# Reordering the prologue of a fused attention and feed-forward kernel: load queues, weights, cluster chain in halves, spread squares, and the place of a normalisation

## The chip, the cores and the metric

The kernel runs on one core of one Trainium2 chip. The metric is the device time of one execution in microseconds (us). A run's "span" comes from its profile and is some 2 us shorter than its time. The profile also gives the mean clock that TensorE was granted, as a share of full speed. Engines in the profile: PE is TensorE (PEld its weight loads), DVE is VectorE, ACT is ScalarE, POOL is GpSimd, SPq is the issuing queue of SyncE, ACTq that of ScalarE.

## The reference, cut to what matters

```python
# q, k, v: 4 batches x 8 heads x 768 positions x 64; 16 centroids per head
q_assign = argmax(q_n @ c_n, clusters);  k_assign = argmax(k_n @ c_n, clusters)
scores   = where(q_assign == k_assign, q @ k.T / 8, -1e9)
x        = softmax(scores) @ v                      # -> 3072 rows of 512
xn       = x / sqrt(mean(x * x) + 1e-6) * rms_g
out      = (silu(xn @ w_gate) * (xn @ w_val)) @ w_out   # 512 -> 1536 -> 512
```

## The kernel before

The kernel keeps q and k transposed, with extra rows below the 64 of the head: 16 rows that mark the position's cluster (one-hot), and one constant row. One product then gives score plus mask. `trans` transposes on TensorE, copies on ScalarE and casts on VectorE and GpSimd. `scores_c` finds the cluster of every position on VectorE and sends the one-hot rows into place by eight small DMAs for a group of four heads.

```python
def load(n):                       # all from SyncE: q, k, v of one head
    ...
    nc.sync.dma_start(out=qk[:, :, 0], in_=src(q))
    nc.sync.dma_start(out=qk[:, :, 1], in_=src(k))
    nc.sync.dma_start(out=vs, in_=src(v))

def trans(g, h, part):
    ...                            # 3 transposes, copy to qkT (one buffer)
    if part:
        nc.gpsimd.tensor_copy(qext[g % 4][:D, h], qkT[g][:D, h])
        nc.vector.tensor_scalar_mul(kext[g % 4][:D, h], qkT[g][D:, h], 1.0 / ZS)
        nc.gpsimd.tensor_copy(vbf[g % 4][:, h, :, :D], vs)
        load(g * HG + h + NSTG)    # the next load, before the rows of oh below

def scores_c(g, m):
    ...                            # 4 products, transpose, max, is_equal, transpose -> oh
        for h in range(HG):
            nc.sync.dma_start(out=qext[g % 4][D:D + NC, h], in_=oh[32 * h:32 * h + NC])
            nc.sync.dma_start(out=kext[g % 4][D:D + NC, h], in_=oh[32 * h + NC:32 * h + 2 * NC])

def rms(u):                        # normalisation of a unit
    for t in range(HT):            # 3 squares with a sum, 512 columns, on ScalarE
        nc.scalar.activation(junk, x[:, t], ACT.Square, accum_out=ss[:, t:t + 1])
    ...                            # 12 tiny VectorE operations: 1/sqrt by Newton
    for t in range(HT):
        nc.vector.tensor_scalar_mul(xn[u][:, t], x[:, t], y[:, t:t + 1])
```

The body is a loop over eight units of half a batch. Between the 24 score steps of unit u it works off a list: the output product of unit u-2, then the feed-forward part of u-1, with the transposes of a later group mixed in.

```python
def ffn_work(u):
    w = [(0.18, lambda c=c: xtrans(u, c)) for c in range(CC)]   # transposes of xn
    ...                                                         # gate and value products
...
for u in range(NU):
    ...
    for h in range(H):
        for i in range(3):
            scores(u, h, i)                                     # 2 products, one exp
            if i == 0 and (u, h) != (0, 0):
                pv(u, h - 1) if h else pv(u - 1, H - 1)
                if h == 0:
                    rms(u - 1)                                  # at the unit's start
            ...                                                 # take from the list
```

The softmax here doesn't subtract the row's maximum and nothing guards it: scores larger than these inputs give would overflow.

## Time and profile before

| | before |
|---|---|
| time, median of 3 runs before the change was measured | 423.85 us (419.03 to 425.24) |
| span of the profiled run, granted clock | 422.2 us, 0.931 |
| first score product | 53.18 us |
| last product of unit 0 with v | 81.2 us |
| first gate product | 90.45 us |
| end of the last unit's products with v (start of the next product) | 381.74 us |

The four instants cut the span into five parts: a prologue to the first scores, unit 0, the wait for the first normalised rows, a body of 291.3 us (90.45 to 381.74) and a tail of 40.5 us. The body holds units 1 to 7. The profile's own lines are in the prediction.

### The profile page before, as it was taken

How to read it: one execution, taken by the hardware profiler on the slowest of the kernel's cores; microseconds unless marked ns; L12 is line 12 of the kernel's file. 1: busy time of each engine (PE TensorE's matmuls, PEld its weight loads, DVE VectorE, ACT ScalarE, POOL GpSimd, SP SyncE). 2: the span in 40 equal slices, each digit the busy share in tenths (PEclk: the TensorE clock that was granted, in tenths of full speed). 3: DMA queues.
4: the chain of work that ended last, by engine and by line, in shares of the span. 5: the costliest groups of instructions: out<-in, count | busy, mean ns of one | idle time of the engine just before them, and what ended most of it. 6: DMA issues, size and time to landing. Idle time of an engine off the chain costs nothing.

```text
span 422.2 us, 7646 instructions
## 1 busy us (share of the span) xinstructions
PE 354.2 (84%) x2995; PEld 213.8 (51%) x3009; DVE 232.4 (55%) x509; ACT 237.7 (56%) x404; POOL 59.6 (14%) x85
## 2 busy tenths in 40 slices
PE   3701188579997999799988999799979999999896
PEld 2301136346754665456635665466546665664452
DVE  4500133555674666756766668567765656666341
ACT  3300259838855676557745774677656675674230
POOL 3840305102110121002300211013100000000000
PEclk9965559869998999999999999999999999999899
DMA  7999985604222233014312220200011001000101
GB/s 188 202 207 207 221 186 144 158 12 98 71 57 70 81 94 79 19 76 110 84 40 89 63 51 2 70 25 2 2 44 50 2 2 75 2 2 13 63 0 75
DMA packets 63795, 32.03 MB, mean 76 GB/s; under 512 B 52976, under 2 KB 59664, under 8 KB 63760
## 3 DMA queue, kind: packets, MB, share of 16 engines
q1 hardware_dynamic: 61024, 26.83, 25.0%
q0 software_dynamic: 2736, 4.72, 6.1%
q8 instruction: 23, 0.38, 0.4%
q14 instruction: 12, 0.10, 0.1%
HBM read 28.35 MB, written 6.29 MB: 82 GB/s over the span
## 4 chain that ended last, share of the span: by engine, by line
PE 69%; DMA 9%; DVE 7%; ACT 6%; SPq 4%; issue 3%; POOL 0%; DVEq 0%; ACTq 0%
PE gate L275 15%; PE val L275 14%; PE s L205 13%; PE o L299 11%; PE acc L221 8%; DMA qk<-in_k_dram 6%; PE tq L160 4%; ACT pT L207 3%; ACT junk L237 2%; PE sc L177 2%; SPq L80 1%; PE tx L264 1%; DVE o_sb L302 1%; DMA vs<-in_v_dram 1%; SPq L81 1%
## 5 line engine op out<-in xcount | busy, mean ns | idle before, releaser
L207 ACT ACTIVATE pT<-s 128x768 bf16<-128x768 f32 x192 | 153.7, 811 | 63.0 <-PE s L205 61.8
L205 PE MATMUL s<-qext,kext 81*128 81x384 bf16 x384 | 96.1, 334 | 17.0 <-issue 7.5
L275 PE MATMUL gate<-xnT,wg 128*128 128x384 bf16 x384 | 80.4, 330 | 0.0
L275 PE MATMUL val<-xnT,wv 128*128 128x384 bf16 x384 | 79.1, 328 | 0.0
L285 DVE SCALAR_TENSOR_TENSOR gu<-th,gate 128x384 f32<-128x384 f32 x84 | 46.5, 553 | 54.0 <-ACT th L283 53.5
L299 PE MATMUL o<-wo,gvT 128*128 128x512 bf16 x274 | 70.5, 388 | 0.8
L163 POOL CAST qext<-qkT 64x768 bf16<-64x768 f32 x32 | 33.9, 1061 | 236.4 <-ACT qkT L161 236.4
L205 PEld LDWEIGHTS <-kext 81*128 81x128 bf16 x384 | 35.9, 99 | 54.5 <-issue 28.3
L160 PE MATMUL tq<-ident_f,qk 128*128 128x128 f32 x192 | 35.5, 308 | 31.2 <-DMA qk<-in_k_dram 30.8
L161 ACT COPY qkT<-tq 128x384 f32<-128x384 f32 x64 | 30.5, 481 | 50.7 <-PE tq L160 49.7
L221 PEld LDWEIGHTS <-pT 128*128 128x128 bf16 x1152 | 46.9, 99 | 12.6 <-ACT pT L207 3.5
L221 PE MATMUL acc<-vbf,pT 128*128 128x65 bf16 x1152 | 50.6, 195 | 2.0 <-ACT pT L207 1.5
L283 ACT ACTIVATE th<-gate 128x384 f32<-128x384 f32 x84 | 41.1, 489 | 19.9 <-PE gate L275 19.9
L290 DVE SCALAR_TENSOR_TENSOR gvT<-gu,val 128x384 bf16<-128x384 f32 x84 | 46.5, 554 | 9.5 <-PE val L275 3.1
L275 PEld LDWEIGHTS <-wv 128*128 128x128 bf16 x384 | 36.7, 98 | 23.1 <-issue 1.4
L275 PEld LDWEIGHTS <-wg 128*128 128x128 bf16 x384 | 36.5, 98 | 22.7 <-issue 1.9
L164 DVE TENSOR_SCALAR kext<-qkT 64x768 bf16<-64x768 f32 x32 | 23.2, 729 | 43.3 <-ACT qkT L161 42.2
L160 PEld LDWEIGHTS tq<-ident_f,qk 128*128 128x128 f32 x192 | 25.9, 157 | 39.8 <-issue 30.1
L299 PEld LDWEIGHTS <-gvT 128*128 128x128 bf16 x288 | 27.3, 99 | 28.5 <-issue 2.6
L237 ACT ACTIVATE junk<-x 128x512 bf16<-128x512 f32 x24 | 15.1, 629 | 18.7 <-DVE x L227 18.2
L302 DVE COPY o_sb<-o 128x512 f32<-128x512 f32 x24 | 16.1, 687 | 11.4 <-PE o L299 9.5
L165 POOL CAST vbf<-vs 128x384 bf16<-128x384 f32 x32 | 18.7, 584 | 0.0
(53 smaller groups left out, 165.0 us busy)
## 6 DMA issues: line engine op xcount, KB each, us to landing
qk<-in_q_dram SPq DMA_DIRECT2D x32, 192.0 KB
qk<-in_k_dram SPq DMA_DIRECT2D x32, 192.0 KB
vs<-in_v_dram SPq DMA_DIRECT2D x32, 192.0 KB
out_dram<-o_sb SPq DMA_DIRECT2D x24, 256.0 KB
wg<-in_moe_w_gate_dram POOLq DMA_DIRECT2D x4, 384.0 KB, 9.0
wv<-in_moe_w_val_dram POOLq DMA_DIRECT2D x4, 384.0 KB, 10.5
wo<-in_moe_w_out_dram POOLq DMA_DIRECT2D x3, 512.0 KB, 19.1
qext<-oh SPq DMA_DIRECT2D x32, 24.0 KB
```

The lines of the kernel that those rows point to most:

```text
L160: nc.tensor.transpose(ps[:, i * P:(i + 1) * P], qk[:, t].rearrange("p a d -> p (a d)"), ident_f)
L161: nc.scalar.copy(qkT[g][:, h, part * UQ:(part + 1) * UQ], ps)
L163: nc.gpsimd.tensor_copy(qext[g % 4][:D, h], qkT[g][:D, h])
L205: nc.tensor.matmul(ps[:, j, :UQ], lhsT=kext[g % 4][:KR, hh, kc * P:(kc + 1) * P], rhs=qext[g % 4][:KR, hh, hf * UQ:(hf + 1) * UQ], start=T ...
L207: nc.scalar.activation(pT[u, h][:, 2 * i:2 * i + 2], ps[:, :, :UQ], ACT.Exp, scale=scale * ZS)
L221: nc.tensor.matmul(acc[:, h % 2, t], lhsT=pT[u, h][:, kc, t * P:(t + 1) * P], rhs=vbf[g % 4][:, hh, kc], start=kc == 0, stop=kc == ST - 1)
L237: nc.scalar.activation(junk, x[:, t], ACT.Square, accum_out=ss[:, t:t + 1])
L275: nc.tensor.matmul(ps, lhsT=w[:, c, f * P:(f + 1) * P], rhs=xnT[u][:, c], start=c == 0, stop=c == CC - 1)
L283: nc.scalar.activation(th, ps, ACT.Tanh, scale=0.5)
L285: nc.vector.scalar_tensor_tensor(gu, th, 1.0, ps, op0=ALU.add, op1=ALU.mult)
L290: nc.vector.scalar_tensor_tensor(gvT[u][:, f], gates[u], 0.5, ps, op0=ALU.mult, op1=ALU.mult)
L299: nc.tensor.matmul(outs[u], lhsT=gvT[u][:, f, t * P:(t + 1) * P], rhs=wo[:, f], start=f == 0, stop=f == FC - 1)
```

## The change

It means to end the 30 us in which TensorE waits for loads, and to take the squares out of the exps' way. Its parts:

1. q and k of the first heads first, k and the first v from ScalarE's queue; later loads after the cluster rows; weights in pieces.
2. The first group's cluster chain in two halves of two heads.
3. The constant row becomes exp's bias: 80 rows, eight small DMAs less.
4. The squares' first 384 columns move between the last head's exps. The rest, and the whole normalisation, move from the unit's start to the list, just ahead of the transposes of xn.
5. Eight dummy products at the very start.

```diff
-        nc.sync.dma_start(out=qk[:, :, 0], in_=src(q))
-        nc.sync.dma_start(out=qk[:, :, 1], in_=src(k))
-        nc.sync.dma_start(out=vs, in_=src(v))
+    nc.sync.dma_start(out=staged[n][:, :, 0], in_=src(q, n))
+    (kq or nc.sync).dma_start(out=staged[n][:, :, 1], in_=src(k, n))
 ...
+    for n in range(HG):
+        load_qk(n, nc.scalar)
+    for n in range(HG, NQ):
+        load_qk(n)
+    for n in range(HG):
+        load_v(n, nc.scalar)
 ...
+    for i in range(WARM):
+        nc.tensor.matmul(warm_ps[:, i % 2], lhsT=warm[:, :P], rhs=warm, start=True, stop=True)
 ...
-    nc.scalar.activation(pT[u, h][...], ps[:, :, :UQ], ACT.Exp, scale=scale * ZS)
+    nc.scalar.activation(pT[u, h][...], ps[:, :, :UQ], ACT.Exp, bias=off, scale=scale * ZS)
 ... (squares(u, t, last): 384 columns early, 128 in rms)
-        w = [(0.18, lambda c=c: xtrans(u, c)) for c in range(CC)]
+        w = [(0.0, lambda: rms(u))] + [(0.18, lambda c=c: xtrans(u, c)) for c in range(CC)]
 ...
+        if h % 2:
+            for m in range(2):
+                scores_c(0, m, h - 1, h + 1)
 ...
+    load_gv(1)
+    load_gv(3)
     for u in range(NU):
 ...
+            def more():
+                for c in range(0, FC, 4):
+                    load_o(c)
+                for n in range(H, H + NV):
+                    if n < H + NQ:
+                        load_qk(n)
+                    load_v(n)
+            fill = first[4:] + [(0.0, more)] + prep
+        elif u == 1:
+            fill = prep[:4] + spread(ffn_work(0), prep[4:])
 ...
-                    if h == 0:
-                        rms(u - 1)
+                if h == H - 1:
+                    squares(u, i, False)
```

More of the change, by code (lines that the diff above doesn't have):

```diff
@@ L50 @@
     scale = 1.0 / (D ** 0.5)
-    KR = D + NC + 1
-    NSTG = 6
+    KR = D + NC
+    WARM = 8
+    NQ, NV = 6, 8
     ctx.enter_context(tc.manual_schedule())
@@ L56 @@
     const = pool("const", 1)
-    stage = pool("stage", NSTG)
+    stage = pool("stage", NQ)
     qk32 = pool("qk32", 1)
@@ L67, with src, load_qk, load_v @@
     ps_g = pool("ps_g", 3, space=PSUM)
-    staged = {}
-    def load(n):
+    staged, stagedv = {}, {}
+    def src(a, n):
+        b, h = divmod(n, H)
+        return a[b, h].rearrange("(p t) d -> p t d", t=ST)
+    def load_qk(n, kq=None):
         if n >= B * H:
             return
-        b, h = divmod(n, H)
-        qk = stage.tile([P, ST, 2, D], F32, tag="qk", name="qk")
-        vs = stage.tile([P, ST, D], F32, tag="vs", name="vs")
-        src = lambda a: a[b, h].rearrange("(p t) d -> p t d", t=ST)
-        nc.sync.dma_start(out=qk[:, :, 0], in_=src(q))
-        nc.sync.dma_start(out=qk[:, :, 1], in_=src(k))
-        nc.sync.dma_start(out=vs, in_=src(v))
-        staged[n] = (qk, vs)
+        staged[n] = stage.tile([P, ST, 2, D], F32, tag="qk", name="qk")
+        nc.sync.dma_start(out=staged[n][:, :, 0], in_=src(q, n))
+        (kq or nc.sync).dma_start(out=staged[n][:, :, 1], in_=src(k, n))
+    def load_v(n, vq=None):
+        if n >= B * H:
+            return
+        stagedv[n] = stage.tile([P, ST, D], F32, tag="vs", name="vs", bufs=NV)
+        (vq or nc.sync).dma_start(out=stagedv[n], in_=src(v, n))
     c_in = const.tile([P, D], F32)
     nc.sync.dma_start(out=c_in, in_=centroids.rearrange("h c d -> (h c) d"))
-    for n in range(NSTG):
-        load(n)
-    gcol = const.tile([P, CC], F32)
-    nc.sync.dma_start(out=gcol, in_=moe_rms_g.rearrange("(c p) -> p c", p=P), allow_slow_non_contiguous=True)
+    for n in range(HG):
[4 more added lines that the diff above has]
+        load_v(n, nc.scalar)
+    gcol = const.tile([P, CC], F32)
+    warm = const.tile([P, 512], BF16)
+    nc.vector.memset(warm, 1.0)
+    warm_ps = ps_s.tile([P, 2, 512], F32, tag="s", name="warm")
+    for i in range(WARM):
+        nc.tensor.matmul(warm_ps[:, i % 2], lhsT=warm[:, :P], rhs=warm, start=True, stop=True)
     ones = const.tile([P, P], F32)
@@ L108 @@
     kext = [const.tile([P, HG, S], BF16, name=f"kext{i}") for i in range(4)]
-    cq = const.tile([1, S], BF16)
-    ck = const.tile([1, S], BF16)
-    nc.gpsimd.memset(cq, -1.0)
-    nc.gpsimd.memset(ck, 1.0)
-    for i in range(4):
-        nc.sync.dma_start(out=qext[i][KR - 1:KR], in_=cq.unsqueeze(1).broadcast_to([1, HG, S]))
-        nc.sync.dma_start(out=kext[i][KR - 1:KR], in_=ck.unsqueeze(1).broadcast_to([1, HG, S]))
     vbf = [const.tile([P, HG, ST, D + 1], BF16, name=f"vbf{i}") for i in range(4)]
@@ L118 @@
         nc.gpsimd.memset(vbf[i][:, :, :, D:D + 1], 1.0)
+    off = const.tile([P, 1], F32)
+    nc.gpsimd.memset(off, -scale * ZS)
     c_sq = const.tile([P, D], F32)
@@ L141, with load_gv, load_o @@
     wo = const.tile([P, FC, DM], BF16)
-    def load_weights():
-        for c in range(CC):
-            nc.gpsimd.dma_start(out=wg[:, c], in_=moe_w_gate[c * P:(c + 1) * P])
-            nc.gpsimd.dma_start(out=wv[:, c], in_=moe_w_val[c * P:(c + 1) * P])
-        for c in range(0, FC, 4):
-            nc.gpsimd.dma_start(out=wo[:, c:c + 4], in_=moe_w_out[c * P:(c + 4) * P].rearrange("(c p) f -> p c f", p=P))
+    def load_gv(c):
+        nc.gpsimd.dma_start(out=wg[:, c], in_=moe_w_gate[c * P:(c + 1) * P])
+        nc.gpsimd.dma_start(out=wv[:, c], in_=moe_w_val[c * P:(c + 1) * P])
+    def load_o(c):
+        nc.gpsimd.dma_start(out=wo[:, c:c + 4], in_=moe_w_out[c * P:(c + 4) * P].rearrange("(c p) f -> p c f", p=P))
     qkT = {}
@@ L155, in trans @@
             qkT[g] = qk32.tile([P, HG, S], F32, tag="qkT", name="qkT")
-        qk, vs = staged[g * HG + h]
+        qk = staged[g * HG + h]
         ps = ps_g.tile([P, UQ], F32, tag="gen", name="tq")
@@ L164, in trans, with vcast @@
             nc.vector.tensor_scalar_mul(kext[g % 4][:D, h], qkT[g][D:, h], 1.0 / ZS)
-            nc.gpsimd.tensor_copy(vbf[g % 4][:, h, :, :D], vs)
-            load(g * HG + h + NSTG)
+    def vcast(n):
+        nc.gpsimd.tensor_copy(vbf[n // HG % 4][:, n % HG, :, :D], stagedv[n])
     scT = {}
-    def scores_c(g, m):
-        if m == 0:
-            scT[g] = asg.tile([P, S], F32, tag="scT", name="scT")
-        ps = ps_g.tile([P, UQ], F32, tag="gen", name="sc")
-        h0 = g * HG % H
-        for h in range(HG):
-            nc.tensor.matmul(ps[32 * h:32 * h + 32], lhsT=cblk[:, h0 + h], rhs=qkT[g][:, h, m * UQ:(m + 1) * UQ],
-                             start=True, stop=True)
-        nc.vector.transpose(scT[g][:, m * UQ:(m + 1) * UQ], ps)
-        if m:
-            n = 2 * S // 32
-            cl = scT[g].rearrange("p (n c) -> p n c", c=NC)
-            mx = small.tile([P, n], F32, tag="mx", name="mx")
-            nc.vector.tensor_reduce(mx, cl, axis=AX, op=ALU.max)
-            ohT = asg.tile([P, S], BF16, tag="ohT", name="ohT")
-            nc.vector.tensor_tensor(ohT.rearrange("p (n c) -> p n c", c=NC), cl,
-                                    mx.unsqueeze(2).broadcast_to([P, n, NC]), op=ALU.is_equal)
-            oh = asg.tile([P, S], BF16, tag="oh", name="oh")
-            nc.vector.transpose(oh, ohT)
-            for h in range(HG):
@@ new lines, with scores_c @@
+    ohs = {}
+    def scores_c(g, m, h0=0, h1=HG):
+        ps = ps_g.tile([P, UQ], F32, tag="gen", name="sc")
+        r = slice(32 * h0, 32 * h1)
+        for h in range(h0, h1):
+            nc.tensor.matmul(ps[32 * h:32 * h + 32], lhsT=cblk[:, g * HG % H + h],
+                             rhs=qkT[g][:, h, m * UQ:(m + 1) * UQ], start=True, stop=True)
+        sct = asg.tile([P, UQ], F32, tag="scT", name="scT", bufs=2)
+        nc.vector.transpose(sct[r], ps[r])
+        n = UQ // NC
+        cl = sct[r].rearrange("p (n c) -> p n c", c=NC)
+        mx = small.tile([P, n], F32, tag="mx", name="mx")
+        nc.vector.tensor_reduce(mx[r], cl, axis=AX, op=ALU.max)
+        ohT = asg.tile([P, UQ], BF16, tag="ohT", name="ohT", bufs=2)
+        nc.vector.tensor_tensor(ohT[r].rearrange("p (n c) -> p n c", c=NC), cl,
+                                mx[r].unsqueeze(2).broadcast_to([32 * (h1 - h0), n, NC]), op=ALU.is_equal)
+        if m == 0:
+            ohs[g, h0] = asg.tile([P, S], BF16, tag="oh", name="oh", bufs=2)
+        oh = ohs[g, h0]
+        nc.vector.transpose(oh[r, m * UQ:(m + 1) * UQ], ohT[r])
+        if m:
+            for h in range(h0, h1):
@@ L206, in scores @@
                              rhs=qext[g % 4][:KR, hh, hf * UQ:(hf + 1) * UQ], start=True, stop=True)
-        nc.scalar.activation(pT[u, h][:, 2 * i:2 * i + 2], ps[:, :, :UQ], ACT.Exp, scale=scale * ZS)
+        nc.scalar.activation(pT[u, h][:, 2 * i:2 * i + 2], ps[:, :, :UQ], ACT.Exp, bias=off, scale=scale * ZS)
     xs, accs = {}, {}
@@ L230, with squares @@
     xn = {}
+    sq = {}
+    def squares(u, t, last):
+        if (t, last) == (0, False):
+            sq[u] = small.tile([P, 2, HT], F32, tag="ss", name="ss")
+        c = slice(DM - 2 * D, DM) if last else slice(0, DM - 2 * D)
+        junk = ffn.tile([P, DM], BF16, tag="junk", name="junk", bufs=1)
+        nc.scalar.activation(junk[:, c], xs[u][:, t, c], ACT.Square, accum_out=sq[u][:, int(last), t:t + 1])
     def rms(u):
         x = xs[u]
-        ss = small.tile([P, HT], F32, tag="ss", name="ss")
         for t in range(HT):
-            junk = ffn.tile([P, DM], BF16, tag="junk", name="junk", bufs=1)
-            nc.scalar.activation(junk, x[:, t], ACT.Square, accum_out=ss[:, t:t + 1])
+            squares(u, t, True)
+        ss = small.tile([P, HT], F32, tag="sm", name="sm")
+        nc.vector.tensor_add(ss, sq[u][:, 0], sq[u][:, 1])
         ms = small.tile([P, HT], F32, tag="ms", name="ms")
@@ L304, in out_mm, with group_work, second @@
             nc.sync.dma_start(out=rows[:, hf * HT + t], in_=o)
-    def group_work(g):
+    def group_work(g, loads=True):
         w = []
         for h in range(HG):
-            for part in range(2):
-                w.append((0.25, lambda h=h, part=part: trans(g, h, part)))
+            n = g * HG + h
+            w.append((0.25, lambda h=h: trans(g, h, 0)))
+            def second(h=h, n=n):
+                trans(g, h, 1)
+                vcast(n)
+                if loads:
+                    load_qk(n + NQ)
+                    load_v(n + NV)
+            w.append((0.25, second))
         for m in range(2):
@@ L336, in out_work @@
         return [(0.86, lambda t=t, p=p: out_mm(u, t, p)) for t in range(HT) for p in range(3)]
-    for _, f in group_work(0):
-        f()
-    load_weights()
-    for _, f in group_work(1)[:2 * HG]:
-        f()
+    for h in range(HG):
+        for part in range(2):
+            trans(0, h, part)
+        if NQ + h < H:
+            load_qk(NQ + h)
+        if h % 2:
+            for m in range(2):
+                scores_c(0, m, h - 1, h + 1)
+    for n in range(HG, H):
+        load_v(n)
+    for h in range(HG):
+        vcast(h)
+        if h % 2:
+            load_gv(h - 1)
+    nc.sync.dma_start(out=gcol, in_=moe_rms_g.rearrange("(c p) -> p c", p=P), allow_slow_non_contiguous=True)
+    first = group_work(1, False)
+    for _, f in first[:4]:
+        f()
+    load_gv(1)
+    load_gv(3)
     for u in range(NU):
@@ L347 @@
             fill += out_work(u - 2)
-        prep = []
+        prep = group_work(u + 2) if u + 2 < NG else []
         if u == 0:
-            fill = group_work(1)[2 * HG:]
-            prep = group_work(2)
-        elif u + 2 < NG:
-            prep = group_work(u + 2)
-        fill += spread(ffn_work(u - 1), prep) if u >= 1 else prep
+            def more():
[4 more added lines that the diff above has]
+                        load_qk(n)
+                    load_v(n)
+            fill = first[4:] + [(0.0, more)] + prep
+        elif u == 1:
+            fill = prep[:4] + spread(ffn_work(0), prep[4:])
+        else:
+            fill += spread(ffn_work(u - 1), prep)
         total = sum(c for c, _ in fill)
@@ L370 @@
     pv(NU - 1, H - 1)
-    rms(NU - 1)
     for _, f in out_work(NU - 2) + ffn_work(NU - 1) + out_work(NU - 1):
```

## The prediction

> **What bounds the kernel now.** I read the page first (busy shares, slices, chain), then the work of the engines in chosen stretches, then the timeline of three places where TensorE stands still.
>
> ```profile
> PE 354.2 (84%) x2995; PEld 213.8 (51%) x3009; DVE 232.4 (55%) x509; ACT 237.7 (56%) x404; POOL 59.6 (14%) x85
> PE   3701188579997999799988999799979999999896
> DMA  7999985604222233014312220200011001000101
> ```
>
> The kernel works in eight units of half a batch: unit u does 24 score/exp steps, and with them the feed-forward part of unit u-1 and the output product of u-2. The second line as slices of 10.55 us: TensorE is empty in slices 3 to 5 and nearly full after slice 9, so the body is TensorE's. In the third line the DMA engines are full in just those empty slices.
>
> ```profile
> core 0: us, PE busy (x) PEld busy (x) DVE busy (x) ACT busy (x) POOL busy (x), PEclk, DMA share, GB/s
> 21.00:32.00 11.00, 0.00 (x0) 0.00 (x0) 0.99 (x2) 0.00 (x0) 4.86 (x8) 0.64 1.09 207
> 42.00:53.00 11.00, 2.04 (x9) 1.26 (x7) 1.11 (x2) 3.12 (x5) 3.33 (x4) 0.50 1.11 218
> 84.00:95.00 11.00, 7.46 (x53) 4.93 (x54) 6.36 (x22) 3.77 (x8) 0.50 (x1) 0.62 0.06 13
> ```
>
> Columns are stretch, length, busy us by engine, granted clock, DMA share, GB/s. From 21 to 53 us nothing runs but loads. The chain of waits and the timeline say which:
>
> ```profile
> 21.01 19.86 DMA qk<-in_k_dram
> 49.55 3.59 DMA kext<-oh
> 53.18 0.82 PE s L205 x2
> ```
>
> ```profile
> 31.27 10.68 SPq L81 DMA_DIRECT2D vs<-in_v_dram  x1
> ```
>
> (chain: start, us, what; the second fence is SyncE's own queue, whose issue of a v load is held for 10.68 us.) The load of head 6's k was issued at 21.0 and landed at 40.9. The cluster rows (oh) of the first four heads had been ready at 20.9 but are issued at 48.9, behind those loads in SyncE's order. So scores begin at 53.2. Unit 0 then ends at 81.2; TensorE next waits for the normalisation (square sums on ScalarE, 13 little VectorE operations), and the first gate product comes at 90.45.
>
> In the body one wait returns at each unit's start (timeline, 127.99 to 130.25):
>
> ```profile
> 127.97 0.63 ACT L237 ACTIVATE junk<-x 128x512 bf16<-128x512 f32 x1
> 129.36 1.49 ACT L207 ACTIVATE pT<-s 128x768 bf16<-128x768 f32 x2
> 130.25 0.80 PE L205 MATMUL s<-qext,kext 81*128 81x384 bf16 x2 [2.25 <-issue]
> 138.68 0.69 DVE L302 COPY o_sb<-o 128x512 f32<-128x512 f32 x1
> ```
>
> Three squares in a row hold ScalarE for 2.25 us, the exps wait behind them, and TensorE stops 2.25 us, at units 2 to 6 (12.7 us idle in their stretches). The 0.80 for two score products instead of 0.49 shows that TensorE came back at half its clock; with it, units 2 and 3 lose some 1.5 us each. The last line matters below: the third output copy is done after the normalisation, which has finished 5 us earlier.
>
> **What the Trainium skill says.** "DMA: Bandwidth & Descriptors", section "Queues, rings and completion order": each engine takes turns between the rings that have work, packet by packet. The trace agrees and gives sizes: gate and value weights have 3072-byte rows, wo 1024, q and k 256 (128 x 6 rows of 64 floats). At 207 GB/s over 16 engines a 3072-byte packet takes 0.237 us, one of 256 about 0.02. While gate/value weights flow, a q or k load (48 packets per engine) so takes 48 x 0.257 = 12.3 us, with wo 48 x 0.098 = 4.7. Test: weights from 17.5, 64 packets per engine, end near 34; by then q6 is in; k6 takes 4.7 with wo, lands at 39 to 40.5. Seen: 40.9. Same page, "Issuing engines are not separate DMA queues": a second issuer only saves issue time; the 0.6 us an issue in the trace is below the 0.8 us a load takes. "TensorE: Matmul & The Clock Gate", "Part 1: The HAM clock gate": idle halves the clock, a few us of work restore it. The trace agrees: clock 0.50 from 32 to 53 us. "ScalarE: Activation LUTs", "What ACT_TABLE_LOAD costs": a pointer operand adds some 93 ns to an ACTIVATE. No run here shows whether exp's constant bias costs that now; it would be at most 192 x 0.093 = 18 us of ScalarE, which is 56% busy.
>
> **The change, part by part.**
>
> Loads and first scores. q and k of heads 0 to 3 go first, from two queues, v later. From the cadence of the old loads (q+k+v 2.45 us) I take 0.93 for a q or k, 0.6 for a v: eight land by about 10.8 (k3 was 13.0). But ScalarE issues eight loads before its table load and the root for the centroids, and the last of these waits for an earlier load (about 8.5). So root at 10.5, centroids transposed at 11.3, and as this stands first on TensorE, transposes of head 0 begin at 11.4 instead of 5.7. The eight dummy products end at about 4.5, so TensorE is cold again. Transposes of heads 0, 1 till 14.4, their cluster scores till 15.9, then VectorE: per half 0.58 + 3 x 0.5 = 2.1, twice, to 19.7. The rows go out at 19.7, land near 23 (2.5 to 3.6 as before). First scores at 23 instead of 53.2: 30 us earlier.
>
> Unit 0. This is where I see most given back. On TensorE the transposes of group 2 (head 8 on) follow two score steps after group 1's last cluster scores (about 32, since ScalarE needs 9 exps x 0.81 and 4 copies x 0.48). But the loads of head 8 are issued only after the eight row DMAs of group 1: 32 + 2.2 VectorE + 8 x 0.62 = 39.2. By then the weights are in flight: first half issued at 22 (16 us of ring in all for gate/value, 8 for wo), the second after v5 is in, about 33, wo at 38 to 41; the ring is busy until 46 to 49. q8 and k8 share it, so k8 lands at 46 to 52. TensorE waits there 12 to 18 us. From head 8's transposes to the unit's end it was 63.2 to 81.2, 18 us; ScalarE's count gives 18 again (14 x 0.81 + 8 x 0.48 + 3 squares x 0.73). So unit 0 ends at 64 to 70, mean 67: 14 us earlier, not 30. Then the wait for the normalisation is 2 to 3 us less (12 transposes fill it, the last squares are 128 wide, 1.3 instead of 2.25). Sum: **-17 us**.
>
> Body. The squares of the first 384 columns move between the exps of the last head: the 2.25 us stop at the start goes away, worth 12.7 idle + 3 of slow clock = 15.7 us in units 2 to 6. But the normalisation moves too: in the built order VectorE now does it after the third output copy, which waits for the last output product, and the next thing on TensorE is the transposes of the normalised rows. From the rows of the profile: copy 0.2 + 0.69, 13 small operations x 0.2 = 2.6, first row block 0.43, two more 0.85, less 0.3 for transposes in between: TensorE idle 3.8, late by 4.3 us. That is in units 2 to 7: 6 x 4.3 = 26. If every stop makes the clock fall (at 1.8 each) it is 36; I take half, 31. Body: 31 - 16 = **+15 us**. At the end the same order delays the last gates: they follow the last output product by 3.4 us now, by about 6: **+3 us**.
>
> Constant row in exp's bias: 81 rows become 80, product time is by columns (384), so nothing; eight small DMAs go away, 5 us of SyncE issue, already in the times above.
>
> Sum: 423.9 - 17 + 15 + 3 = 424.9; I say **424 us**, one less for the two favourable rivals below.
>
> **The rivals.** First: head 8's loads land early, no stop in unit 0. For it: DMA work is the same in sum and starts earlier. Against: the ring arithmetic hits k6 within 1 us. Unit 0 would end at about 50, TensorE another 14 to 17 us ahead: 408. Second: the normalisation is not exposed, because something else covers it; then the body gains 13 to 16 and the time is 400 to 405 with my prologue. Against: engine order is fixed, and nothing stands between the last output product and the transposes. Third: every stop makes the clock fall and the weights starve the loads longer: +5 and +5, 434. Fourth: the bias does cost 93 ns; ScalarE sets the pace in unit 0 (14 exps, 1.3 us) and where squares and exps mix, +2 to +4.
>
> **Range and chances.** The two large terms are opposed, each good to some 8 us, and both of the favourable rivals lie below: 406 to 435 holds 8 of 10. Faster than 415.4 needs one of the first two rivals: 0.33. Slower than 432.3 needs the third: 0.2. Between: 0.47.
>
> **What would show it.** Right: first scores near 23 us; an idle TensorE of 10 us or more before the group 2 transposes with the releaser a q or k load; first gate near 75; at each of units 2 to 7 an idle of 3.5 us or more before the transposes of xn, released by VectorE, and no 2.25 us stop at the unit's start; squares of 384 and 128 columns; exp at 0.81 or 0.90. Wrong: group 2 transposes without a wait, or an idle before xn's transposes under 1 us.

## The result, and the profile after

The changed kernel is slower: 447.89 us median of 4 runs (447.31 to 448.44) against 422.75 of 4 runs of the kernel before in the same rounds (419.03 to 425.24). The ratio is 1.060, 95% interval 1.052 to 1.069. Here and below a ratio is the mean time of one kernel's fast runs over that of the kernel before's fast runs of the same rounds, so it is not quite the ratio of the medians quoted. All eight runs here were fast.

The same instants in both profiles (us), with the prediction's value:

| | before | after | change | predicted |
|---|---|---|---|---|
| first score product | 53.18 | 25.15 | -28.0 | -30 |
| last product of unit 0 with v | 81.2 | 74.7 | -6.5 | -14 |
| first gate product | 90.45 | 85.31 | -5.1 | -17 |
| body, first gate to last product with v | 291.3 | 318.1 | +26.8 | +15 |
| tail, from there to the end | 40.5 | 43.3 | +2.8 | +3 |

Together -5.1 + 26.8 + 2.8 = +24.5, which is the spans' difference (446.7 - 422.2).

The page of the kernel after, busy times of the engines, then TensorE and the DMA engines in 40 slices of 11.2 us:

```profile
PE 370.0 (83%) x3003; PEld 223.9 (50%) x3017; DVE 249.0 (56%) x550; ACT 257.1 (58%) x452; POOL 57.9 (13%) x84
...
PE   4793086699969998799969996999959995997896
...
DMA  9598998422022422224113002000100010001001
```

The empty slices 3 to 5 of before have shrunk to slices 4 and 5. But a 6 or 5 now returns every four or five slices in the body, where before had 7 to 9. The instructions are nearly the same in number and TensorE is busy 16 us longer: it works more slowly.

**Prologue.** The chain of waits of the kernel after (start, us, what):

```profile
39.06 5.33 DMA qext<-oh
45.10 10.63 DMA qk<-in_k_dram
```

and its timeline (start, us, engine, line, operation, idle before it and what ended that):

```profile
55.87 0.87 PE L171 MATMUL tq<-ident_f,qk 128*128 128x128 f32 x3 [17.34 <-DMA qk<-in_k_dram]
```

The stop was predicted: head 8's k is issued behind eight row DMAs, and takes 10.63 us while weights flow beside it (a k load's median here is 3.7; experiment 4 tests this cause). By then these are the output weights: the last gate and value loads land at 45.2, the three of w_out at 48.8, 51.9 and 55.3. TensorE stands for 17.34 us. In the windows table of the same kernel, columns as in the prediction, the first row is that stop:

```profile
core 0: us, PE busy (x) PEld busy (x) DVE busy (x) ACT busy (x) POOL busy (x), PEclk, DMA share, GB/s
40.00:56.00 16.00, 0.13 (x1) 0.17 (x2) 0.00 (x0) 0.00 (x0) 1.75 (x3) 0.58 1.17 209
...
128.00:132.00 4.00, 0.35 (x2) 0.00 (x0) 3.46 (x16) 1.00 (x6) 0.00 (x0) 0.90 0.17 66
132.00:136.00 4.00, 3.38 (x19) 2.36 (x19) 2.43 (x7) 1.27 (x2) 0.00 (x0) 0.50 0.00 0
```

The first scores themselves come 2 us later than predicted, with this in the timeline of the kernel after:

```profile
3.57 4.53 ACTq L88 DMA_DIRECT2D vs<-in_v_dram  x4
8.13 1.28 ACT L138 ACT_TABLE_LOAD   x1 [8.13 <-DMA qk<-in_q_dram]
...
19.27 3.07 DVE L175 TENSOR_SCALAR kext<-qkT 64x768 bf16<-64x768 f32 x2
19.27 0.95 POOL L178 CAST vbf<-vs 128x384 bf16<-128x384 f32 x2
...
22.46 0.48 ACT L172 COPY qkT<-tq 128x384 f32<-128x384 f32 x1 [4.39 <-DVE kext L175]
```

ScalarE issues four v loads until 8.1 us before it may take the root for the centroids, as foreseen. Not foreseen: two VectorE casts take 3.07 us beside GpSimd's casts and weight issues, where one alone takes 0.56. The Trainium skill's page "GPSIMD Engine Reference", "1. Specifications", says that GpSimd's SBUF interfaces are shared with VectorE, for some of VectorE's instructions; the slow casts here agree with that, but no run separates it. As qkT has one buffer, the copy for the next group waits 4.39 us for them.

**Body.** The last two rows of the windows table above are the start of unit 2: TensorE all but empty for 4 us, then at half its clock. Its timeline:

```profile
128.39 0.69 DVE L326 COPY o_sb<-o 128x512 f32<-128x512 f32 x1
...
129.10 0.16 DVE L261 TENSOR_TENSOR sm<-ss 128x3 f32<-128x3 f32 x1
...
131.67 1.28 DVE L279 TENSOR_SCALAR xn<-x,ny 128x512 bf16<-128x512 f32 x3
...
132.22 1.40 PE L288 MATMUL tx<-ident,xn 128*128 128x128 bf16 x6 [3.87 <-DVE xn L279]
...
133.41 0.85 PE L220 MATMUL s<-qext,kext 80*128 80x384 bf16 x2
```

VectorE evicts the third output tile first, then does the 13 tiny operations (129.10 to 131.67), then scales the rows. TensorE, in order, has only the transposes of those rows next. After the stop two score products take 0.85 us instead of 0.49. The same stop stands in every unit from 3 on, in the same timeline:

```profile
181.17 0.23 PE L288 MATMUL tx<-ident,xn 128*128 128x128 bf16 x1 [3.86 <-DVE xn L279]
...
229.50 0.23 PE L288 MATMUL tx<-ident,xn 128*128 128x128 bf16 x1 [3.86 <-DVE xn L279]
...
277.75 0.23 PE L288 MATMUL tx<-ident,xn 128*128 128x128 bf16 x1 [3.86 <-DVE xn L279]
...
329.16 1.40 PE L288 MATMUL tx<-ident,xn 128*128 128x128 bf16 x6 [5.24 <-DVE xn L279]
...
374.92 1.40 PE L288 MATMUL tx<-ident,xn 128*128 128x128 bf16 x6 [5.24 <-DVE xn L279]
```

The six sum to 25.9 us of idle, and in the 4 us from each the granted clock is 0.50 to 0.65 on average. The last two, of units 6 and 7, are longer for another reason: the last squares stand on ScalarE behind an exp, and VectorE, done with its copy, waits for them. For unit 6:

```profile
326.04 0.16 DVE L261 TENSOR_TENSOR sm<-ss 128x3 f32<-128x3 f32 x1 [1.72 <-ACT junk L254]
```

### The profile page after: what moved, and what is told of

Its sections match the earlier page's. It is cut to its first block, busy times and chain, and to the rows that moved or that the text cites. A ratio compares the mean times of both kernels' runs of the same rounds, so it can differ in the third digit from the quotient of the medians.

```text
span 446.7 us, 7733 instructions
## 1 busy us (share of the span) xinstructions
PE 370.0 (83%) x3003; PEld 223.9 (50%) x3017; DVE 249.0 (56%) x550; ACT 257.1 (58%) x452; POOL 57.9 (13%) x84
## 4 chain that ended last, share of the span: by engine, by line
PE 67%; DVE 13%; ACT 10%; DMA 6%; issue 3%; SPq 0%; ACTq 0%; DVEq 0%
PE o L323 14%; PE gate L299 13%; PE s L220 12%; PE val L299 12%; PE acc L236 7%; ACT pT L222 6%; PE tq L171 4%; PE sc L189 3%; DMA qk<-in_k_dram 2%; DVE xn L279 2%; DVE kext L175 2%; DMA qk<-in_q_dram 2%; PE tx L288 2%; ACT junk L254 2%; ACT qkT L172 1%
## 5 line engine op out<-in xcount | busy, mean ns | idle before, releaser
L222 ACT ACTIVATE pT<-s,off 128x768 bf16<-128x768 f32 x192 | 172.5, 902 | 87.2 <-PE s L220 86.8
L220 PE MATMUL s<-qext,kext 80*128 80x384 bf16 x384 | 99.9, 345 | 1.7 <-ACT pT L222 1.6
L299 PE MATMUL gate<-xnT,wg 128*128 128x384 bf16 x384 | 83.6, 342 | 0.8 <-DVE xnT L289 0.8
L323 PE MATMUL o<-wo,gvT 128*128 128x512 bf16 x274 | 68.2, 378 | 0.8
L171 PE MATMUL tq<-ident_f,qk 128*128 128x128 f32 x192 | 38.3, 326 | 21.8 <-DMA qk<-in_k_dram 17.3
L220 PEld LDWEIGHTS <-kext 80*128 80x128 bf16 x384 | 38.0, 104 | 35.7 <-issue 12.2
L314 DVE SCALAR_TENSOR_TENSOR gvT<-gu,val 128x384 bf16<-128x384 f32 x84 | 46.5, 554 | 11.8 <-PE val L299 5.1
L299 PEld LDWEIGHTS <-wv 128*128 128x128 bf16 x384 | 37.2, 99 | 23.4 <-issue 1.9
L175 DVE TENSOR_SCALAR kext<-qkT 64x768 bf16<-64x768 f32 x32 | 29.0, 912 | 34.3 <-ACT qkT L172 33.8
L288 PE MATMUL tx<-ident,xn 128*128 128x128 bf16 x96 | 15.4, 300 | 37.2 <-DVE xn L279 36.0
L171 PEld LDWEIGHTS tq<-ident_f,qk 128*128 128x128 f32 x192 | 28.3, 169 | 32.3 <-issue 19.1
L326 DVE COPY o_sb<-o 128x512 f32<-128x512 f32 x24 | 16.6, 692 | 37.5 <-PE o L323 37.2
L288 PEld LDWEIGHTS <-xn 128*128 128x128 bf16 x96 | 9.9, 133 | 44.5 <-DVE xn L279 43.5
```

The source lines that it names most:

```text
L171: nc.tensor.transpose(ps[:, i * P:(i + 1) * P], qk[:, t].rearrange("p a d -> p (a d)"), ident_f)
L220: nc.tensor.matmul(ps[:, j, :UQ], lhsT=kext[g % 4][:KR, hh, kc * P:(kc + 1) * P], rhs=qext[g % 4][:KR, hh, hf * UQ:(hf + 1) * UQ], start=T ...
L222: nc.scalar.activation(pT[u, h][:, 2 * i:2 * i + 2], ps[:, :, :UQ], ACT.Exp, bias=off, scale=scale * ZS)
L288: nc.tensor.transpose(ps[:, t * P:(t + 1) * P], xn[u][:, t, c * P:(c + 1) * P], ident)
L299: nc.tensor.matmul(ps, lhsT=w[:, c, f * P:(f + 1) * P], rhs=xnT[u][:, c], start=c == 0, stop=c == CC - 1)
L314: nc.vector.scalar_tensor_tensor(gvT[u][:, f], gates[u], 0.5, ps, op0=ALU.mult, op1=ALU.mult)
```

## The experiments

Four theories were to be told apart. A: the late normalisation costs the body's 27 us and more. B: exp's bias costs some of it. C: the weights, sharing the DMA engines, hold back head 8's loads. D: the dummy products or the squares matter. The runs came in three groups (experiments 1 to 4, 5 to 8, 9 to 12), each on another chip and beside its own 7 runs of the kernel before (medians 423.65, 421.42 and 420.69 us). Of these, none, three and one fell in the slow state, and so did two runs of experiment 6 and one of experiment 9; medians and ranges below are of all runs, ratios of the fast ones. Between groups, compare ratios or the parts of a profile: a difference of a few us in time can be the chip's or the run's.

### 1. The normalisation back at the unit's start

The kernel after, with the 384-column squares still spread.

```diff
-        w = [(0.0, lambda: rms(u))] + [(0.18, lambda c=c: xtrans(u, c)) for c in range(CC)]
+        w = [(0.18, lambda c=c: xtrans(u, c)) for c in range(CC)]
 ...
                     pv(u, h - 1) if h else pv(u - 1, H - 1)
+                    if h == 0:
+                        rms(u - 1)
 ... (and rms(NU - 1) after the loop)
```

> The changed kernel with one thing undone: the normalisation stands again at the start of a unit (right after the last head's value product) and not behind the output copies; the squares stay split and spread. Theory A (the late normalisation leaves TensorE without work before the transposes of xn, six times in the body and once at the end, 3.9 to 5.5 us idle each and half clock after it): the stops before xn's transposes fall to under 1 us, the way from the first gate to the last block of output products, 318 us in the changed kernel, falls to 285 to 292, the time from 448 to 415 to 422. Rival B (the body is slower because exp takes 0.90 instead of 0.81 us and the squares are twice as many instructions, ScalarE being the pace): the stops may go but the time falls by less than 10 us.

Measured: 410.41 us (410.14 to 410.91), ratio 0.972 (0.964 to 0.980). The first gate stays at 85.4; the body falls from 318.1 to 281.1, 37.0 less, and is 10.2 shorter than in the kernel before. The start of unit 2 in its timeline:

```profile
124.75 1.28 DVE L279 TENSOR_SCALAR xn<-x,ny 128x512 bf16<-128x512 f32 x3
...
129.25 1.02 PE L323 MATMUL o<-wo,gvT 128*128 128x512 bf16 x4
...
130.11 0.50 PE L288 MATMUL tx<-ident,xn 128*128 128x128 bf16 x6
130.31 0.69 DVE L326 COPY o_sb<-o 128x512 f32<-128x512 f32 x1
130.45 0.49 PE L220 MATMUL s<-qext,kext 80*128 80x384 bf16 x2
```

The rows are ready 5 us before TensorE comes to them; no idle stands before the transposes, and the score products keep their 0.49 us. Theory A is shown, and is larger than expected. The 37.0 are 25.9 us of idle and a rest of 11.1 us, slow work behind the six stops: TensorE's busy time in the body falls by 11.5 us (287.6 to 276.1), its mean clock there rises from 0.94 to 0.99. Unit 2 as an example: from the first transposes to the first value product it is 132.22 to 138.13 after, 5.9 us; here the same instructions take 3.3 (130.11 to 133.10, and 0.32 for a block of transposes that comes one place later).

### 2. The kernel before with only the normalisation moved

```diff
-        w = [(0.18, lambda c=c: xtrans(u, c)) for c in range(CC)]
+        w = [(0.0, lambda: rms(u))] + [(0.18, lambda c=c: xtrans(u, c)) for c in range(CC)]
 ...
-                    if h == 0:
-                        rms(u - 1)
 ... (and rms(NU - 1) after the loop)
```

> The kernel before with this one thing added: the normalisation, squares and all, moved behind the output copies, ahead of xn's transposes. Theory A: it loses nearly all that the changed kernel lost in the body: the 2.25 us stops at the units' starts go, stops of 4 to 6 us with slow clock come in units 2 to 7 and at the end; 422 becomes 443 to 452. Rival B (exp and square instructions): nothing of that is in here, 422 stays within 5 us.

Measured: 454.49 us (453.44 to 456.49), ratio 1.077 (1.069 to 1.084), above the 443 to 452 expected. The first gate is at 90.2 as before, the body 321.3 instead of 291.3. So the move alone costs 30 us, with none of the other parts in the kernel. In its waits (who waited for whom: us, times, longest) stands

```profile
PE tx L264 <- DVE xn L255: 40.5, 10, 6.0
```

where the kernel before has

```profile
PE tx L264 <- DVE xn L255: 6.0, 1, 6.0
```

### 3. The kernel before with only the constant row in exp's bias

```diff
-    KR = D + NC + 1
+    KR = D + NC
 ...
-        nc.scalar.activation(..., ACT.Exp, scale=scale * ZS)
+        nc.scalar.activation(..., ACT.Exp, bias=off, scale=scale * ZS)
```

> The kernel before with only the constant row moved into exp's bias (80 rows, no eight small DMAs). Theory A: exp goes from 0.81 to 0.90 us, 17 us more ScalarE time that hides behind TensorE; the loads of head 6 are issued some 5 us earlier as the eight small DMAs are gone; time within 4 us of before, 419 to 426. Rival B: ScalarE sets the pace, the time rises by 10 us or more.

Measured: 427.57 us (424.51 to 428.03), ratio 1.011 (1.003 to 1.018), a little above the expected range. The costliest group of the page, in the kernel before and in this one (busy us, mean ns of one, idle before):

```profile
L207 ACT ACTIVATE pT<-s 128x768 bf16<-128x768 f32 x192 | 153.7, 811 | 63.0 <-PE s L205 61.8
```

```profile
L202 ACT ACTIVATE pT<-s,off 128x768 bf16<-128x768 f32 x192 | 170.7, 901 | 62.1 <-PE s L200 61.4
```

Each exp takes 90 ns longer, 17 us of ScalarE in all. The first scores come 1.7 us earlier (51.4), the body is 2.8 us longer (294.1). So the bias costs about 1%: it makes ScalarE 17 us busier and some 3 us of that reach the end. The row of 81 costs TensorE nothing that could be seen: the median score product takes 326 ns with 81 rows and with 80.

### 4. The weights later

The kernel after, with half of the gate and value weights and all of w_out issued only after group 2's casts.

```diff
-    load_gv(1)
-    load_gv(3)
 ...
-                for c in range(0, FC, 4):
-                    load_o(c)
 ...
-            fill = first[4:] + [(0.0, more)] + prep
+            fill = first[4:] + [(0.0, more)] + prep[:8] + [(0.0, weights)] + prep[8:]
```

> The changed kernel with the second half of the gate and value weights and all of wo issued after group 2's casts instead of before group 2's loads. Theory C (weight packets of 3072 and 1024 bytes take turns with the 256-byte packets of q and k and starve them): head 8's k, issued at 45.1, lands at 48 to 49.5 instead of 55.8, TensorE's stop before group 2's transposes falls from 17.3 to 10 or 11 us, and the time falls by 5 to 8 us, unless the weights now come too late for the first gates. Rival D (the landing is late only because it is issued late and the queue is long): k lands at 54 or later and the time stays within 2 us.

Measured: 443.53 us (440.13 to 443.67), ratio 1.048 (1.040 to 1.056), 4.4 us under the kernel after where 5 to 8 were expected. Head 8's k is issued at 44.89, nearly as after, and landed about 4 us later instead of 10.6:

```profile
48.89 0.87 PE L171 MATMUL tq<-ident_f,qk 128*128 128x128 f32 x3 [10.59 <-DMA qk<-in_k_dram]
```

The stop is 6.8 us shorter, the first gate comes at 80.3 instead of 85.3. Theory C is shown, but it is only 7 of the 17 us: the other 10.6 are the late issue, with the load's own 4 us.

### 5. Loads of the next batch ahead of the row DMAs

Experiments 1 and 4 together, and q and k of heads 8 to 11 issued before group 1's cluster rows.

```diff
     for _, f in first[:4]:
         f()
+    for n in range(H, H + HG):
+        load_qk(n)
 ...
-                    if n < H + NQ:
+                    if H + HG <= n < H + NQ:
                         load_qk(n)
```

> Normalisation at the unit's start (410.4 us), the second half of the weights late, and q and k of heads 8 to 11 issued right after the transposes of heads 4 and 5, ahead of group 1's eight row DMAs, not behind them. Theory C with the order of issue: the stop before group 2's transposes (16.6 us there) goes to under 2 us, unit 0 ends near 56 instead of 75, the first gate comes at 62 to 68 and the time at 388 to 394. Rival (the DMA engines are full anyway, and what is loaded earlier is missed later): rows or weights come late in turn, first gate at 74 or later, time 399 or more.

Measured: 398.32 us (395.02 to 400.75), ratio 0.947 (0.938 to 0.956). The times lie in two pairs, near 395.6 and 400.6; the profile is of the faster pair. In its timeline the transposes of group 2 (first line) follow without a wait, and the only stop for a k load is in unit 1:

```profile
38.46 0.52 PE L171 MATMUL tq<-ident_f,qk 128*128 128x128 f32 x3
...
72.31 0.87 PE L171 MATMUL tq<-ident_f,qk 128*128 128x128 f32 x3 [2.70 <-DMA qk<-in_k_dram]
```

So the stop before group 2 was the order of issue plus the sharing with the weights, and nothing else. Unit 0 ends at 57.7 and the first gate is at 68.1, about as expected. The time is not: 388 to 394 were expected. The rival is right in part, as late loads come back elsewhere: group 1's rows land late (a stop of 2.11 us at 42.4), and head 14's k, issued at 53.05 beside the weights, takes 19.1 us and holds up unit 1 by the 2.70 us above. With 398 us this beats both kernels.

### 6. The first v loads from SyncE instead of ScalarE

```diff
-        load_v(n, nc.scalar)
+        load_v(n)
```

> The same with the four first v loads issued by SyncE and not by ScalarE. If ScalarE's waits in these issues hold the centroids' root (8.1 to 9.6 us in the changed kernel) and with it all transposes, the root comes at 4 to 5 us, first transposes at 5 to 6, first scores 3 to 5 us earlier and the time falls by 2 to 5 us against the run without this. Rival (q and k of heads 0 to 3 are not all in before 10.8, so the cluster chain cannot start much earlier): less than 1.5 us.

Measured: 398.09 us (394.42 to 401.07), ratio 0.939 (0.934 to 0.945), against the 398.32 of experiment 5. Again two runs are near 395 and two near 401 (here these two are classed slow, there they just are not), so there is no difference. Its profile fell into a slow execution, so only its prologue is read. The transposes begin at 5.8 us, 4.5 earlier, but the first scores come at 28.1, not earlier. The waits show where the gain went:

```profile
PE s L220 <- DMA kext<-oh: 11.5, 2, 10.2
```

The rows are ready sooner but land late, behind loads that now stand in the same queue: the four v loads push head 7's k back, it is issued at 14.25 just ahead of the first weights (14.53) and takes 13.4 us (3.3 in experiment 5), and the rows issued behind it from 15.74 on take 10 to 12 us. A wait on ScalarE was changed into a wait on a DMA.

### 7. Without the dummy products, on experiment 1

```diff
-    WARM = 8
+    WARM = 0
 ... (and the line that allocates their tile)
```

> Normalisation at the unit's start, without the eight dummy products. They end at 5.0 us and real work begins at 10.1, so the clock has fallen again: no difference, 409 to 412. Rival (the clock is kept up by them): the transposes of heads 0 to 3 take longer and the time rises by 1 us or more.

Measured: 406.37 us (406.06 to 406.55), ratio 0.966 (0.963 to 0.970), 4 us under experiment 1, which was on another chip; by the ratios it is 0.6%, some 2.4 us, and the intervals overlap. That is more than expected. But both profiles agree to 0.4 us up to the last product with v (366.1 and 366.5). They part in the tail, at the third output tile. First the timeline of experiment 1, then that of this one:

```profile
377.60 0.69 DVE L326 COPY o_sb<-o 128x512 f32<-128x512 f32 x1 [3.64 <-DMA out_dram<-o_sb]
378.34 0.65 PE L288 MATMUL tx<-ident,xn 128*128 128x128 bf16 x6 [3.56 <-DVE o_sb L326]
```

```profile
375.18 0.69 DVE L325 COPY o_sb<-o 128x512 f32<-128x512 f32 x1 [1.59 <-DMA out_dram<-o_sb]
375.92 0.65 PE L287 MATMUL tx<-ident,xn 128*128 128x128 bf16 x6 [1.50 <-DVE o_sb L325]
```

The copy waits for a store to free one of two output tiles. Why that store lands 2 us sooner here stays open; experiments 9 and 10 take the wait away and ask again.

### 8. Whole squares at the unit's start, on experiment 1

```diff
-                if h == H - 1:
-                    squares(u, i, False)
 ...
+            nc.scalar.activation(junk, x[:, t], ACT.Square, accum_out=ss[:, t:t + 1])
 ... (and the sum of the two parts)
```

> Normalisation at the unit's start as in the kernel before, the squares whole again: three of 512 columns in a row at the start of a unit, nothing between the last exps. If the split and spread squares are what gains the 10 us of the body (291 us before, 281 with the normalisation at the start), the 2.25 us stops come back in units 2 to 6 and the time rises from 410.4 to 418 to 423. Rival (the gain comes from the cluster chain in halves, which frees VectorE earlier): 410 to 413.

Measured: 416.58 us (415.75 to 417.72), ratio 0.991 (0.987 to 0.995), just under the 418 to 423 expected. The stops before the exps of units 2 to 6 come back, but at 1.1 to 1.7 us. The body is 287.9 us, 6.8 longer than in experiment 1 (4.7 of idle, 2.1 of busy time). So spreading the squares is worth 6.8 us; the rest of the body's gain over the kernel before, 291.3 - 287.9 = 3.4 us, comes from the other parts, net of the bias.

### 9. A third output tile, on experiment 5

```diff
-    outp = pool("outp", 2)
+    outp = pool("outp", 3)
-    ones = const.tile([P, P], F32)
+    ones = const.tile([P, 32], F32)     # only makes room; 32 columns are used
```

> The kernel with early loads, late weights and the normalisation at the unit's start, but with three output tiles instead of two. Theory T (in the tail the third output copy waits for the first tile's store, 3.6 us on VectorE, and TensorE's transposes behind it 3.5 us; that stop then halves the clock): the copy's wait for the store goes to 0, the transposes' wait for the copy goes, tail (last product with v to the end) about 38 instead of about 42 us, 393-396 us. Rival (the transposes wait for the normalisation chain anyway, which ends about when the copy does): under 1 us off, 397-399.

Measured: 396.12 us (392.10 to 398.52), ratio 0.936 (0.928 to 0.945). The copies no longer wait for a store, and of TensorE's wait for them is left

```profile
PE tx L288 <- DVE o_sb L326: 0.4, 1, 0.4
```

instead of 3.5 us. The tail is 37.2 us (353.0 to 390.2) instead of 41.9 in experiment 5. Theory T is shown in the profile; in the times the gain of 2 us lies within the spread of the runs. The profiles also differ where nothing was changed: the first gate is at 72.4 here and at 68.1 in experiment 5, the body 280.6 and 284.3 us.

### 10. The same without dummy products

> As the one with three output tiles, without the dummy products. Theory N (the dummies do nothing: the centroid transpose waits for the root until 10 us in either, and what the earlier run without them gained lay in the tail, in the wait for a store): within 1 us of the kernel with them, and the two traces equal to 0.5 us at the first scores. Rival (the dummies cost something by themselves that the tail only showed): 3-4 us faster than with them.

The edit is that of experiment 7. Measured: 396.25 us (396.00 to 396.49), ratio 0.940 (0.934 to 0.945): the time of experiment 9 as far as its spread (392.10 to 398.52) lets one tell. The centroid transpose is at 11.4 us in both, and both tails are 37.2 us. So no effect of the dummies on the time can be seen; one of 2 or 3 us would not show. The second half of theory N failed: the first scores come at 29.0 instead of 26.5, a difference larger than 0.5 us that the medians don't show. With one profile of each it can't be put down to the dummies.

### 11. Unit 1's list rearranged, on experiment 9

```diff
-            fill = prep[:4] + spread(ffn_work(0), prep[4:])
+            fill = prep[:8] + spread(ffn_work(0), prep[8:])
```

> As the one with three output tiles, with all eight transposes of group 3 (instead of four) ahead of unit 0's normalised tiles in unit 1's list. Theory W (the stop of 3.6 us before unit 0's normalised tiles is a plain wait for VectorE's chain of 17 small operations, during which 12 transposes and two scores can be done): the stop falls under 1.5 us and the whole gains 2-3 us against the kernel with three output tiles. Rival (the work is only moved; TensorE is short elsewhere, and the copies of the four more tiles stand ahead of exps on ScalarE): 0-1 us.

Measured: 400.76 us (398.21 to 401.81), ratio 0.949 (0.941 to 0.956): 4.6 us slower than experiment 9, though the two intervals just overlap. The wait for VectorE is gone from its waits, but its timeline has

```profile
80.33 0.87 PE L171 MATMUL tq<-ident_f,qk 128*128 128x128 f32 x3 [9.01 <-DMA qk<-in_k_dram]
```

With a stop of 3.69 us just before, the first gate moves from 72.4 to 85.4. The transposes that were to fill the 3.6 us need heads whose loads run beside the weights at that time (DMA share 1.22 and 1.17 in the ten us before). Both theories miss: the work was there, its data was not.

### 12. The constant row back, on experiment 11

The diff is experiment 3's, reversed, with the two constant rows written into a tile of the exps' pool.

> As the one with group 3's transposes moved, with the constant row back in q's and k's extensions (81 rows) and no bias in exp. Theory B (bias costs 91 ns on each of 192 exps, ScalarE 17 us of busy time, of which about 2-4 us reach the end, as the kernel before with the bias alone showed at +4): 2-4 us faster, exp at 811 ns. Rival (eight more small transfers at the start, and ScalarE is not the bound): 0-1 us or slower by 1-2, first scores later.

Measured: 398.71 us (398.23 to 399.10), ratio 0.946 (0.940 to 0.951), 2 us under experiment 11, with exp at 811 ns. That is the low end of theory B. The two intervals overlap, so the size rests on experiment 3; the sign is the same in both.

The best is experiment 9 (or 10, without the dummies): 396 us, 6% under the kernel before and 12% under the kernel after.

## Why the prediction was wrong

The prediction had 424 us and at most 435; it is 448. Every wait that it named is in the profile, and the direction of each term but one is right. Three of its terms were mis-sized, the body by 11.8 us and the two before it together by 11.9.

**The body, +15 predicted, +26.8 measured: the largest single error.** "6 x 4.3 = 26" was right in sum: six stops, 25.9 us of idle. In part that is luck: it had 3.8 us of idle and 4.3 of lateness each; four stops are 3.86 or 3.87, but two are 5.24, by a wait of VectorE for ScalarE's squares that it did not have. The step that failed is "If every stop makes the clock fall (at 1.8 each) it is 36; I take half, 31". Every stop made it fall, and with the stops that cost 37.0 (experiment 1). The third rival had this. The other side of the sum, the 2.25 us stop "worth 12.7 idle + 3 of slow clock = 15.7", was too large: the whole rest of the change shortens the body by 10.2 (291.3 to 281.1), of which the squares are 6.8 (experiment 8). Part of the gap is the bias, which the prediction counted as nothing in its sum and which adds 2.8 (experiment 3); that was the fourth rival. So 37.0 - 10.2 = 26.8 in place of 31 - 16 = 15.

**Unit 0, -14 predicted, -6.5 measured.** The chain was right: late issue behind eight row DMAs, sharing with the weights, a stop of 12 to 18 us. The step that failed is "32 + 2.2 VectorE + 8 x 0.62 = 39.2" for head 8's issue. The increments held (2.6 us of VectorE, 5.2 for eight issues); the 32 did not. Group 1's last cluster scores end at 36.5 in the trace: 2 us of it are the late first scores, and 1.3 the table load before the first exp (ACT_TABLE_LOAD, 25.89 to 27.17), which the sum left out. So the rows go out from 39.06 and head 8's k, behind its q, at 45.1. The DMA engines were also busy for longer, with w_out until 55.3 and not until 46 to 49. The load landed at 55.7, not by 52. From there to the unit's end it is 18.9 us for the predicted 18. Experiments 4 and 5 take one cause and then both away, and the stop falls to 10.6 us and to nothing.

**The normalisation after unit 0, "2 to 3 us less" predicted, 1.3 longer measured** (10.6 for 9.3). The spread squares do end earlier, but in the list the four copies of the next group and an exp stand ahead of the last three. In experiment 1, where they do not, VectorE starts on its tiny operations 1.5 us sooner (77.31 for 78.85), but the rows start at 81.61 as in the kernel after (81.62), and the first gate is at 85.4. Its timeline shows why: four of the tiny operations take 0.42 to 0.81 us instead of 0.16, each ending with one of GpSimd's casts. So the order on ScalarE alone was not the limit, and what would shorten this wait stays open. Experiment 11 tried to fill the stop and failed for want of data.

First scores (2 us off) and tail (+2.8 for +3) were right. So was the answer to the second rival: nothing covers the normalisation, as the order on the engines is fixed. The range was too narrow: it set two large opposed terms against each other at some 8 us each, and each missed by 12 in the same direction. Even the two unfavourable rivals together, 434 and +2 to +4, stay under 448.

Two readings of its lines were loose, without effect on the outcome: the DMA engines are full in slices 2 to 6 and not only in 3 to 5, and the kernel before has 12 tiny VectorE operations and not 13. Its arithmetic of the shared DMA engines also counts one row as one packet, where the page cited lets a packet hold several descriptors; it hit head 6's k, and no run here tests the difference.

## What to carry to other kernels

Put the small, serial chain that an in-order engine will need next as early as its inputs allow; moving it next to its consumer cost 30 to 37 us here, five to six in each of six units. When counting stops of TensorE as long as these (3.9 us and more), add the slow clock behind every one: 11 us on top of 26. And before moving loads or transposes, check who shares the DMA engines at that time: the same k load took 10.6 us beside the weights and 4 without, and weights put off to a later place held up the loads there (19.1 us for a k load in experiment 5).

## What the Trainium skill lacked or had wrong

- "DMA: Bandwidth & Descriptors", "Queues, rings and completion order", tells that the engines take turns packet by packet, but not what it does to a load of small rows: 192 KB in rows of 256 bytes beside weights in rows of 1024 bytes took 10.63 us, and about 4 with the weights later, behind the same cluster rows and q load in its own queue.
- "TensorE: Matmul & The Clock Gate", "Part 1: The HAM clock gate", gives some 3.4 us of idling for the fall to half speed. Here all six stops of 3.86 to 5.24 us were followed by it, at a cost of 11.1 us beyond the idle itself. In the kernel before, two of the five stops of 2.2 us were also followed by half clock (units 2 and 3: 0.50 in the 3 us after the first, 0.68 in the 4 us after the second) and three were not (1.00), so a stop shorter than the page's figure can bring it too.
- "ScalarE: Activation LUTs", "What ACT_TABLE_LOAD costs", is right on the pointer operand: 811 became 901 ns. No page says how little of such a cost may reach the end: 17 us of ScalarE became about 3.
